# Attention steps of three blocks placed one slot earlier, and the sums of weights cut into four steps instead of three

## The chip, the cores and the metric

The kernel runs on one core of one Trainium2 chip. The metric is the device time of one execution in microseconds (us). The engines are PE (TensorE: matmuls), DVE (VectorE), ACT (ScalarE), POOL (GpSimd) and SP (SyncE, which issues all DMAs here). Each engine works through its own instructions in the order in which they were written down, and waits where an instruction needs something that another engine has not finished.

## The reference

```python
def _attn_ref(q, k, v):                      # B, H, S, D = 8, 8, 576, 64
    ...                                      # cut into chunks of 64 positions
    scores = scale * np.matmul(q_c, k_c.transpose(0, 1, 2, 4, 3))
    scores = scores - np.max(scores, axis=-1, keepdims=True)
    attn = np.exp(scores)
    attn = attn / (np.sum(attn, axis=-1, keepdims=True) + 1e-09)
    out = np.matmul(attn, v_c)
    ...
def _moe_ref(x, w_in, w_out):                # x: 4608 x 512, w_in: 512 x 2048
    h = x @ w_in
    relu6 = np.clip(h + 3.0, 0.0, 6.0)
    g = h * relu6 / 6.0
    return (g @ w_out).astype(np.float32)
```

Chunked attention (64 x 64 blocks) gives the 4608 x 512 matrix x; two large products with a gate between them give the output, all in 32-bit floats.

## The kernel before, in words

The 4608 rows are nine blocks of 512. Every 32-bit product is made of three matmuls: operands are split into a high part and a low part, and `passes` (lines 221 to 223) adds high·high, high·low and low·high.

**Blocks 0 to 2, the standard part.** Here the two products run directly. A `slot` is half a step: an even slot is `mm1`, 12 matmuls of 128x512 into a PSUM tile `h` (two buffers), and an odd slot is `mm2`, 12 matmuls into four `acc` tiles, for the `g` of two steps earlier (`LAG`). There are 96 slots. After `mm1`, ACT makes `r` from `h` (L233), DVE gates it (L234), ACT casts it to `g` (L235) and DVE takes the rest (L236); these four stand in the queues of ACT and DVE in that order.

**Blocks 3 to 8, the Strassen part.** They run in three pairs by one level of a Strassen scheme, which needs sums and differences of quarters of the weights, high and low parts again. These come from `prepare(m, p)`, 16 units (8 values of p, 2 of m) that run during the standard part, in slots 30 to 83. A unit adds high and low part of two weight tiles into the one buffer `a` (two DVE adds, L337), forms four quarters in place (L347, four DVE operations), casts them to the one buffer `hl` (ACT, L350), takes the low part (DVE, L352), and stores four quarters from `hl` to DRAM (L355). It also stores three quarters that need no sum directly from the weight tiles (L333). `hl` and `a` have one buffer each, so the cast of a unit (L350) waits until the four stores of the unit before have landed.

**Attention of blocks 2, 3 and 4** also runs during the standard part, in six pieces (block and half of the heads), put at slots 30, 38, 52, 60, 68 and 76. A piece loads q and k (L142) and v (L147), does 64 small matmuls for the scores (L154), the softmax in four steps (`soft` 0 and 1: row maximum L161 and subtraction L164 on DVE, exponential L165 on ACT; `soft` 2 and 3: sum L168, L169, reciprocal L170, product L172 on DVE), eight transposes on PE (L183) with a copy back by ACT (`e`, L185), and 64 small matmuls for the values (L194), whose result ACT copies out as `x` (L203 or L200). Scores, transposes and values share one PSUM tile, `two`.

**What sets the order.** From slot 30 the order is written out by hand (`manual_schedule`). The table `later` gives each step's distance from the piece's slot. In each slot the matmuls of `mm1` or `mm2` and their ACT and DVE operations come first, then the planned items of that slot, attention ahead of `prepare` (rank 20), then the pending low part L236. A unit of `prepare` starts every third or fourth slot: 30, 33, 36, 40, 43, 46, 50, 53, 57, 60, 63, 67, 70, 73, 77, 80. In slots 43 and 67 `mm2` ends a block, and its four `acc` tiles are emptied by ACT and DVE.

In the text the six pieces are called places 1 to 6, and "mm1(38)", "L185(39)" mean the instruction of that slot.

Of the kernel before, what the change touches and what calls it, by code (L numbers as in the profile page):

```python
# [8 lines left out]
F32 = mybir.dt.float32  # L9
# [21 lines left out]
NFP = NFT // 2  # L31
# [10 lines left out]
def tile_kernel(ctx: ExitStack, tc: tile.TileContext, qk_in, v_in, weights, out):  # L42
    nc = tc.nc
# [45 lines left out]
    words, w, w_h, w_l = {}, {}, {}, {}  # L89
# [28 lines left out]
    def convert_to(ft):  # L118
        nonlocal converted
        load_to(ft + 3)  # L120
        while converted < min(ft, NFT):
            convert(converted)
            converted += 1
# [91 lines left out]
    def finish():  # L215
        while low:
            low.pop(0)()
# [56 lines left out]
    def moe_slots(n, ft, *seg):  # L274

        g = mm1(n, ft)
        yield
        pending.append((n, ft, g, *seg))
        if len(pending) > LAG:
            mm2(*pending.pop(0))  # L280
        yield
# [35 lines left out]
    def kept(m, p, i):  # L317

        if m:
            return stream_b[i, p // 4][:, p % 4]  # L320
        k = ORDER_A.index(i)
        return stream_a[p, k // 4][:, k % 4]

    def quarter(m, row, col):

        return (col, row) if m else (row, col)

    def prepare(m, p):
        cols = lambda k: slice(256 * k, 256 * k + 256)
        for i, row, col in ((1, 0, 0), (2, 0, 1), (4, 1, 1)):  # L330
            f, k = quarter(m, row, col)
            to = kept(m, p, i).rearrange("p (l t) -> p l t", l=2)
            nc.sync.dma_start(out=to, in_=w[p + NFP * f][:, :, m, cols(k)].bitcast(F32))  # L333
        a = sp.tile([P, 2, 512], F32, name="a")
        for f in range(2):
            h, l = [w[p + NFP * f][:, k, m].bitcast(F32) for k in range(2)]
            DVE.tensor_tensor(out=a[:, f], in0=h, in1=l, op=ALU.add)  # L337
        yield

        def q(row, col):  # L340
            f, k = quarter(m, row, col)
            return a[:, f, cols(k)]


        for to, x, y, op in ((q(1, 1), q(1, 0), q(1, 1), ALU.add), (q(1, 0), q(0, 0), q(1, 0), ALU.subtract),
                             (q(0, 0), q(1, 1), q(0, 0), ALU.subtract), (q(0, 1), q(0, 1), q(0, 0), ALU.subtract)):
            DVE.tensor_tensor(out=to, in0=x, in1=y, op=op)  # L347
        hl = sp.tile([P, 2, 2, 2, 256], F32R, name="hl")
        s = a.rearrange("p f (k t) -> p f k t", k=2)
        ACT.copy(out=hl[:, :, :, 0], in_=s)  # L350
        yield
        DVE.tensor_tensor(out=hl[:, :, :, 1], in0=s, in1=hl[:, :, :, 0].bitcast(F32), op=ALU.subtract)  # L352
        for i, row, col in ((5, 1, 1), (7, 1, 0), (6, 0, 0), (3, 0, 1)):
            f, k = quarter(m, row, col)
            nc.sync.dma_start(out=kept(m, p, i), in_=hl[:, f, k].rearrange("p l t -> p (l t)").bitcast(F32))  # L355
        yield


# [4 lines left out]
    def fetch():  # L363
        if stream:
            t, n = stream.pop(0)
            w = wsp.tile([P, 4, 2, 256], F32R, name="ws")
            nc.sync.dma_start(out=w[:, :n].rearrange("p n l t -> p (n l t)").bitcast(F32), in_=t[:, :n].rearrange("p n t -> p (n t)"))
            ahead.append(w)
# [11 lines left out]
    def x_operands(s, eng):  # L380

        n = NSTD + 2 * s
        b = [[xraw[n + j][:, i] for j in range(2)] for i in range(NDP)]
        sub = lambda out, x, y: eng.tensor_tensor(out=out, in0=x, in1=y, op=ALU.subtract)
        ops[s] = {}
        sub(b[0][1], b[0][1], b[0][0])
        for i in ORDER_A:
            ops[s][i] = operand()
            r, c = WHERE[i]
            split(ops[s][i], b[r][c])  # L390

            if i == 5:
                sub(b[0][1], b[1][1], b[0][1])
            elif i == 6:
                sub(b[0][0], b[0][1], b[0][0])
                sub(b[0][1], b[1][0], b[0][1])
            yield
# [3 lines left out]

    plan = {}
    early = [(0, "load_qk"), (1, "load_v"), (2, "scores"), (2, "softmax"), (7, "transpose"), (10, "values")]
    later = [(-2, "load_qk"), (3, "load_v"), (3, "scores"), (4, "soft", 0), (4, "soft", 1), (5, "soft", 2), (5, "soft", 3),
             (8, "transpose"), (9, "values")]

    def put(n, dp, at, steps, stretch=1.0):
        a = Attention(n, dp)
# [7 lines left out]
    SUMS = first[1] + 22  # L416
    FREE = first[3] + 2 * (NFP + LAG + 1)
    for (n, dp), at in zip(((2, 0), (2, 1), (3, 0), (4, 0), (4, 1), (3, 1)), (30, 38, 52, 60, 68, 76)):
        put(n, dp, at, later)
    for u in range(2 * NFP):  # L420
        for k in range(3):
            plan.setdefault(SUMS + u * (FREE - 2 - SUMS) // (2 * NFP) + k, []).append((20, lambda: next(prep)))
    prep = (step for p in range(NFP) for m in range(2) for step in prepare(m, p))
    slot = 0
    sp = made = None
    order = ExitStack()

    for i, (n, lo, hi) in enumerate(SEGMENTS):
        last = all(m != n for m, *_ in SEGMENTS[i + 1:])
        for ft in range(lo, hi):  # L430
            if i == 0:
                convert_to(min(ft + 2, 4))
            elif slot < SUMS:

                with tc.issue_after(second.done.ins):
                    convert_to(5)
                with tc.issue_after(second.last.ins):
                    convert_to(min(6 + 2 * ft, NFT))
            elif slot == SUMS:
                scratch.close()  # L440
                sums = ExitStack()
                sp = sums.enter_context(tc.tile_pool(name="sp", bufs=1, side="right"))
                op = sums.enter_context(tc.tile_pool(name="op", bufs=4, side="right"))
                order.enter_context(tc.manual_schedule())
            for _ in moe_slots(n, ft, ft == lo, ft == hi - 1, not last):
                for _, f in sorted(plan.pop(slot, []), key=lambda s: s[0]):
                    f()
                finish()
                slot += 1
                if slot == FREE:  # L450
                    assert next(prep, None) is None
                    sums.close()
                    op = None
                    start.close()
                    upper.close()
                    xop_pool = pool("xop", 8, side="right")
                    wsp = pool("wsp", 3, side="right")
                    for _ in range(3):
                        fetch()
                    made = x_operands(0, DVE)  # L460
                elif slot > FREE:
                    next(made, None)
# [197 lines left out]
```

## Time and profile before

| what | us |
|---|---|
| median of three runs (lowest, highest) | 855.14 (854.91, 855.72) |
| the profiled execution, whole | 855.06 |
| its span, first to last instruction | 853.1 |
| PE busy in the span | 814.5 |
| DVE busy | 635.8 |
| ACT busy | 369.1 |
| POOL busy | 132.0 |

The span is what the profiler sees between the first and the last instruction; about 2 us of the execution lie outside it. The standard part with the hand-written order begins at 123.9 us (mm1(30)); attention's last values step ends at 322.1 us (slot 85); the Strassen part begins at 354.9 us. In a timeline row stand the start, the duration, the engine, the line, the operation, what is written and read, how many instructions are merged, and in brackets the idle time of that engine just before and what ended it. Matmuls overlap: one of 128x512 has a row of 0.39 us, but the next starts about 0.23 us after it.

### The profile page before, as it was taken

The numbers are of one execution on the slowest core, as the hardware profiler recorded it, in microseconds if no ns is written. First come the engines' busy times: TensorE is split into PE (matmuls) and PEld (weight loads), VectorE is DVE, ScalarE is ACT, GpSimd is POOL, SyncE is SP. The second block draws the span as 40 slices with busy tenths as digits, with TensorE's granted clock in tenths as the row PEclk, the third lists the DMA queues.
The fourth block names the chain that finished last, engine by engine and source line by source line (L and its number), as shares of the span: only waits on it lengthen the run. The fifth ranks groups of instructions, "written<-read, shape, count | busy, mean of one in ns | idle before, by whom it ended". The sixth has DMA issues, their size and how long they took to land.

```text
span 853.1 us, 13690 instructions
## 1 busy us (share of the span) xinstructions
PE 814.5 (95%) x5683; PEld 658.7 (77%) x5683; DVE 635.8 (75%) x768; ACT 369.1 (43%) x455; POOL 132.0 (15%) x77
## 2 busy tenths in 40 slices
PE   7889999789998999999999999999999999999998
PEld 5766878568776777878878888788788887887886
DVE  5978997585866776487699946876899466669951
ACT  4747763243334334334455443344554333336330
POOL 0000000000001000022227002222370022326200
PEclk9898999899999999999999999999999999999999
DMA  9893003856768745166655576666554765555563
GB/s 365 315 360 120 13 0 112 247 184 214 220 187 296 237 160 196 60 232 226 244 189 191 229 254 228 233 214 245 204 192 167 234 226 178 207 186 197 197 212 134
DMA packets 50014, 172.86 MB, mean 203 GB/s; under 512 B 4640, under 2 KB 16928, under 8 KB 39200
## 3 DMA queue, kind: packets, MB, share of 16 engines
q1 hardware_dynamic: 49952, 171.99, 58.0%
q8 instruction: 45, 0.74, 0.3%
q14 instruction: 17, 0.14, 0.1%
HBM read 133.17 MB, written 38.80 MB: 202 GB/s over the span
## 4 chain that ended last, share of the span: by engine, by line
PE 67%; DVE 22%; ACT 5%; issue 3%; DMA 2%; POOL 0%; SPq 0%; ACTq 0%; DVEq 0%
PE acc L221 14%; PE acc L223 14%; PE acc L222 14%; PE h L221 7%; PE h L222 7%; PE h L223 7%; PE two L194 2%; DVE xop L373 2%; DVE m L161 2%; DVE r L234 2%; DVE z L168 1%; DMA w<-w_in_out 1%; DVE a L347 1%; DVE e L164 1%; DVE g L496 1%
## 5 line engine op out<-in xcount | busy, mean ns | idle before, releaser
L221 PE MATMUL acc<-xop,ws 128*128 128x512 f32 x528 | 208.6, 396 | 4.4 <-DVE u L484 4.4
L222 PE MATMUL acc<-xop,ws 128*128 128x512 f32 x528 | 205.8, 390 | 0.0
L223 PE MATMUL acc<-xop,ws 128*128 128x512 f32 x528 | 205.4, 390 | 0.0
L221 PEld LDWEIGHTS acc<-xop,ws 128*128 128x128 f32 x528 | 99.1, 188 | 27.6 <-DVE u L484 6.8
L373 DVE TENSOR_TENSOR xop<-g,xop 128x1024 fp32r<-128x1024 f32 x72 | 103.4, 1468 | 21.5 <-ACT xop L372 21.5
L223 PEld LDWEIGHTS acc<-xop,ws 128*128 128x128 f32 x528 | 99.1, 188 | 20.9
L222 PEld LDWEIGHTS acc<-xop,ws 128*128 128x128 f32 x528 | 99.2, 188 | 19.8
L372 ACT CAST xop<-g 128x1024 fp32r<-128x1024 f32 x72 | 74.4, 1051 | 78.9 <-PE acc L223 51.3
L504 POOL TENSOR_TENSOR g<-g 128x512 f32<-128x512 f32 x24 | 34.8, 1449 | 307.3 <-DVE g L496 307.3
L221 PE MATMUL h<-x,w 128*128 128x512 f32 x192 | 80.0, 419 | 2.1 <-ACT x L203 1.2
L222 PE MATMUL h<-x,w 128*128 128x512 f32 x192 | 78.4, 409 | 0.0
L223 PE MATMUL h<-x,w 128*128 128x512 f32 x192 | 77.8, 405 | 0.0
L222 PE MATMUL acc<-g,w 128*128 128x512 f32 x192 | 75.5, 393 | 0.3 <-DVE g L236 0.3
L221 PE MATMUL acc<-g,w 128*128 128x512 f32 x192 | 75.4, 397 | 0.1
L223 PE MATMUL acc<-g,w 128*128 128x512 f32 x192 | 75.4, 393 | 0.0
L234 DVE SCALAR_TENSOR_TENSOR r<-r,h 128x512 f32<-128x512 f32 x48 | 32.8, 683 | 50.7 <-ACT r L233 50.7
L495 ACT ACTIVATE r<-acc,half 128x512 f32<-128x512 f32 x72 | 48.5, 685 | 26.3 <-DVE acc L484 25.4
L495 ACT ACTIVATE r<-h,half 128x512 f32<-128x512 f32 x24 | 16.5, 687 | 95.0 <-DVE h L484 95.0
L222 PE MATMUL h<-xop,ws 128*128 128x512 f32 x144 | 56.2, 390 | 0.2 <-DVE xop L373 0.2
L221 PE MATMUL h<-xop,ws 128*128 128x512 f32 x144 | 56.3, 391 | 0.0
L223 PE MATMUL h<-xop,ws 128*128 128x512 f32 x144 | 56.1, 389 | 0.0
L496 DVE SCALAR_TENSOR_TENSOR g<-r,acc 128x512 f32<-128x512 f32 x72 | 48.6, 683 | 7.0 <-ACT r L495 6.7
(93 smaller groups left out, 1270.5 us busy)
## 6 DMA issues: line engine op xcount, KB each, us to landing
ws<-b SPq DMA_DIRECT2D x42, 1024.0 KB, 4.8
ws<-a SPq DMA_DIRECT2D x24, 1024.0 KB, 4.9
ws<-a SPq DMA_DIRECT2D x24, 768.0 KB, 4.3
qk<-qk_in SPq DMA_DIRECT2D x17, 1024.0 KB, 6.6
w<-w_in_out SPq DMA_DIRECT2D x16, 1024.0 KB, 13.4
v<-v_in SPq DMA_DIRECT2D x17, 512.0 KB, 5.1
a<-hl SPq DMA_DIRECT2D x32, 256.0 KB, 3.4
b<-hl SPq DMA_DIRECT2D x32, 256.0 KB, 3.4
```

The costliest lines, as they stand in the source:

```text
L161: DVE.tensor_reduce(out=self.m, in_=flat(self.s), axis=AX.X, op=ALU.max)
L164: DVE.tensor_tensor(out=flat(self.e), in0=flat(self.s), in1=wide(self.m), op=ALU.subtract)
L194: PE.matmul(po[o, s, a, i, :], lhsT=self.v[rows, a, i, o], rhs=self.aT[rows, a, i, o], start=True, stop=True)
L221: PE.matmul(ps, lhsT=a_h, rhs=b_h, start=first, stop=False, skip_group_check=more)
L222: PE.matmul(ps, lhsT=a_h, rhs=b_l, start=False, stop=False, skip_group_check=more)
L223: PE.matmul(ps, lhsT=a_l, rhs=b_h, start=False, stop=last, skip_group_check=more)
L234: DVE.scalar_tensor_tensor(out=r, in0=r, scalar=1.0, in1=h, op0=ALU.min, op1=ALU.mult)
L372: ACT.copy(out=t[:, :, 0], in_=src)
L373: DVE.tensor_tensor(out=t[:, :, 1], in0=src, in1=t[:, :, 0].bitcast(F32), op=ALU.subtract)
L495: return (lambda: ACT.activation(out=r, in_=ps, func=AF.Relu, bias=half, scale=1.0 / 6.0), lambda: DVE.scalar_tensor_tensor(out=out, in0=r ...
L496: lambda: DVE.scalar_tensor_tensor(out=out, in0=r, scalar=1.0, in1=ps, op0=ALU.min, op1=ALU.mult))
L504: sub = lambda o, x, y: lambda: POOL.tensor_tensor(out=o, in0=x, in1=y, op=ALU.subtract)
```

## The change

Two things change, both in the standard part.

The table of attention steps: every step comes one slot earlier, so that it falls into a slot of the other kind. The scores come after `mm1` instead of after `mm2`, the transposes at the end of an odd slot (after `mm2`) instead of an even one, and the values at the end of the next even slot. `load_v` keeps its slot and comes behind `soft` 0 and 1.

The units of `prepare`: four steps instead of three. The cast to `hl` (ACT) has a step and a slot of its own, so the cast, the low part and the stores all come one slot later. The three stores of untouched quarters come last in the unit, behind the four stores from `hl`, where they stood first. The starting slots of the units stay.

```diff
     def prepare(m, p):
         cols = lambda k: slice(256 * k, 256 * k + 256)
-        for i, row, col in ((1, 0, 0), (2, 0, 1), (4, 1, 1)):
-            f, k = quarter(m, row, col)
-            to = kept(m, p, i).rearrange("p (l t) -> p l t", l=2)
-            nc.sync.dma_start(out=to, in_=w[p + NFP * f][:, :, m, cols(k)].bitcast(F32))
         a = sp.tile([P, 2, 512], F32, name="a")
...
             DVE.tensor_tensor(out=to, in0=x, in1=y, op=op)
+        yield
         hl = sp.tile([P, 2, 2, 2, 256], F32R, name="hl")
...
             nc.sync.dma_start(out=kept(m, p, i), in_=hl[:, f, k].rearrange("p l t -> p (l t)").bitcast(F32))
+        for i, row, col in ((1, 0, 0), (2, 0, 1), (4, 1, 1)):
+            f, k = quarter(m, row, col)
+            to = kept(m, p, i).rearrange("p (l t) -> p l t", l=2)
+            nc.sync.dma_start(out=to, in_=w[p + NFP * f][:, :, m, cols(k)].bitcast(F32))
         yield
...
-    later = [(-2, "load_qk"), (3, "load_v"), (3, "scores"), (4, "soft", 0), (4, "soft", 1), (5, "soft", 2), (5, "soft", 3),
-             (8, "transpose"), (9, "values")]
+    later = [(-3, "load_qk"), (2, "scores"), (3, "soft", 0), (3, "soft", 1), (3, "load_v"), (4, "soft", 2), (4, "soft", 3),
+             (7, "transpose"), (8, "values")]
...
     for u in range(2 * NFP):
-        for k in range(3):
-            plan.setdefault(SUMS + u * (FREE - 2 - SUMS) // (2 * NFP) + k, []).append((20, lambda: next(prep)))
-    prep = (step for p in range(NFP) for m in range(2) for step in prepare(m, p))
+        unit = prepare(u % 2, u // 2)
+        for k in range(4):
+            plan.setdefault(SUMS + u * (FREE - 2 - SUMS) // (2 * NFP) + k, []).append((20, lambda unit=unit: next(unit)))
```

In the changed file the lines of `prepare` are numbered anew: the adds are L333, the quarters L343, the cast L347, the low part L349, the stores from `hl` L352 and those from the weights L356. All other operations of attention and `mm1`, `mm2` keep their line numbers.

The first place to look at is PE's order around the transposes of place 1, as a piece of the difference. `two` is the PSUM tile of attention, `e` the attention weights, `h` the result of `mm1`, `acc` that of `mm2`.

```order
 L222 MATMUL h<-x,w_1049 128x512
 L223 MATMUL h<-x,w_1049 128x512
-L183 MATMUL two<-ident,e 128x128 x8
+L194 MATMUL two<-e,v 64x64 x32
 L221 MATMUL acc<-g,w_998 128x512
 L222 MATMUL acc<-g,w_998 128x512
```

Behind mm1(38), where the transposes stood, the values now stand; the transposes moved ahead of that mm1. One slot of 12 matmuls lies between transposes and values in both kernels, a `mm2` before and a `mm1` now.

ACT's order at the same place, before, from the exponential of slot 34 to the copy of `x`:

```order
L165 ACTIVATE e_1389<-e_1389 128x1024
L350 CAST hl_1396<-a_1366 128x4x256
L233 ACTIVATE r_1434<-h_1421,half_97 128x512
L235 CAST g_1435<-r_1434 128x512
L350 CAST hl_1464<-a_1444 128x4x256
L233 ACTIVATE r_1479<-h_1466,half_97 128x512
L235 CAST g_1480<-r_1479 128x512
L185 COPY e_1389<-two_1484 128x1024
L203 CAST x_1545<-two_1512 128x2x8x64
```

And in the changed kernel:

```order
L165 ACTIVATE e_1355<-e_1355 128x1024
L233 ACTIVATE r_1384<-h_1371,half_97 128x512
L235 CAST g_1385<-r_1384 128x512
L347 CAST hl_1413<-a_1368 128x4x256
L233 ACTIVATE r_1428<-h_1415,half_97 128x512
L235 CAST g_1429<-r_1428 128x512
L185 COPY e_1355<-two_1457 128x1024
L233 ACTIVATE r_1484<-h_1471,half_97 128x512
L235 CAST g_1485<-r_1484 128x512
L203 CAST x_1522<-two_1489 128x2x8x64
```

Before, the copy L185 stands behind L233 and L235 of the same slot's `mm1` and behind a cast to `hl`; now it stands ahead of the next `mm1`'s L233, and the cast to `hl` ahead of it is that of two slots earlier.

The second place is place 6. ACT before, from the exponential to the copy of `e`:

```order
L165 ACTIVATE e_2829<-e_2829 128x1024
L350 CAST hl_2860<-a_2835 128x4x256
L233 ACTIVATE r_2875<-h_2862,half_97 128x512
L235 CAST g_2876<-r_2875 128x512
L233 ACTIVATE r_2911<-h_2898,half_97 128x512
L235 CAST g_2912<-r_2911 128x512
L185 COPY e_2829<-two_2916 128x1024
```

And in the changed kernel:

```order
L165 ACTIVATE e_2799<-e_2799 128x1024
L347 CAST hl_2804<-a_2726 128x4x256
L233 ACTIVATE r_2819<-h_2806,half_97 128x512
L235 CAST g_2820<-r_2819 128x512
L233 ACTIVATE r_2870<-h_2857,half_97 128x512
L235 CAST g_2871<-r_2870 128x512
L347 CAST hl_2875<-a_2837 128x4x256
L185 COPY e_2799<-two_2890 128x1024
```

Here one more cast to `hl`, that of the last unit, comes to stand directly ahead of the copy L185.

DVE in the changed kernel at place 6, from the row maximum on:

```order
L161 TENSOR_REDUCE m_2797<-two_2747 128x16
L164 TENSOR_TENSOR e_2799<-two_2747,m_2797 128x1024
L234 SCALAR_TENSOR_TENSOR r_2819<-r_2819,h_2806 128x512
L168 TENSOR_REDUCE z_2824<-e_2799 128x16
L169 TENSOR_SCALAR z_2824<-z_2824 128x16
L170 RECIPROCAL z_2824<-z_2824 128x16
L172 TENSOR_TENSOR e_2799<-e_2799,z_2824 128x1024
L349 TENSOR_TENSOR hl_2804<-a_2726,hl_2804 128x4x256
L333 TENSOR_TENSOR a_2837<-w7_823 128x512
L333 TENSOR_TENSOR a_2837<-w15_1049 128x512
L236 TENSOR_TENSOR g_2820<-r_2819,g_2820 128x512
L343 TENSOR_TENSOR a_2837<-a_2837 128x256 x4
```

The low part L349 of the last unit but one stands behind both halves of the softmax's second part, and its stores from `hl` are what the last cast L347 waits for.

More of the change, by code (lines that the diff above doesn't have):

```diff
@@ L450, in tile_kernel @@
                 if slot == FREE:
-                    assert next(prep, None) is None
                     sums.close()
```

## The prediction

> **What bounds the kernel now.** I read the busy times by stretch first, cut where the hand-written order begins, where attention ends and where the Strassen part begins.
>
> ```profile
> core 0: us, PE busy (x) PEld busy (x) DVE busy (x) ACT busy (x) POOL busy (x), PEclk, DMA share, GB/s
> 123.89:322.08 198.19, 180.95 (x1488) 146.09 (x1489) 140.08 (x215) 73.21 (x96) 3.11 (x2) 0.97 0.65 203
> 322.08:354.87 32.79, 32.79 (x151) 27.15 (x145) 20.25 (x22) 15.22 (x20) 0.00 (x0) 1.00 0.29 110
> 354.87:853.00 498.13, 489.83 (x3105) 400.21 (x3103) 370.42 (x411) 200.67 (x249) 127.73 (x68) 1.00 0.60 209
> ```
>
> Only the first stretch is touched. PE is idle there for 198.19 - 180.95 = 17.2 us, and its clock is 0.97. The middle stretch holds ten slots and the two last `mm2`, 12 groups of 12 matmuls without a gap: 32.79 / 12 = 2.73 us for a slot, 0.23 for a matmul. Next PE's row in the waits of the first stretch (us in total, times, longest):
>
> ```profile
> PE two L194 <- ACT e L185: 17.1, 6, 6.4
> ```
>
> All the idle time is one wait: the values' matmuls wait for ACT's copy of the transposed weights, once at each place. PE's timeline shows the six:
>
> ```profile
> 149.82 1.03 PE L183 MATMUL two<-ident,e 128*128 128x128 f32 x8
> 150.62 0.48 PE L221 MATMUL acc<-g,w 128*128 128x512 f32 x1
> ...
> 159.95 1.98 PE L194 MATMUL two<-e,v 64*64 64x64 f32 x64 [6.35 <-ACT e L185]
> ...
> 190.25 1.69 PE L194 MATMUL two<-e,v 64*64 64x64 f32 x64 [2.72 <-ACT e L185]
> ...
> 235.31 1.16 PE L194 MATMUL two<-e,v 64*64 64x64 f32 x64 [1.63 <-ACT e L185]
> ...
> 264.14 1.16 PE L194 MATMUL two<-e,v 64*64 64x64 f32 x64 [2.69 <-ACT e L185]
> ...
> 293.31 1.16 PE L194 MATMUL two<-e,v 64*64 64x64 f32 x64 [1.72 <-ACT e L185]
> ...
> 320.99 1.16 PE L194 MATMUL two<-e,v 64*64 64x64 f32 x64 [2.03 <-ACT e L185]
> 322.08 0.50 PE L221 MATMUL h<-x,w 128*128 128x512 f32 x1
> ```
>
> Transposes occupy PE for 0.80 us (149.82 to 150.62), values for 1.09 (320.99 to 322.08). The clock after such a wait stands in the busy times of the values with the 12 matmuls behind them, at places 1, 2, 4 and 6:
>
> ```profile
> 159.95:165.43 5.48, 5.48 (x76) 4.67 (x77) 1.35 (x2) 1.01 (x1) 0.00 (x0) 0.69 1.01 266
> 190.25:195.76 5.51, 5.50 (x77) 4.64 (x77) 3.03 (x6) 2.06 (x2) 0.00 (x0) 0.69 0.83 242
> 264.14:269.68 5.54, 5.54 (x76) 4.52 (x77) 1.93 (x3) 2.06 (x2) 0.00 (x0) 0.69 1.05 388
> 320.99:324.94 3.95, 3.95 (x77) 3.38 (x77) 0.00 (x0) 1.01 (x1) 0.00 (x0) 1.00 0.48 128
> ```
>
> After waits of 2.69 us and more the granted clock is 0.69 and the same work takes 5.48 to 5.54 instead of 3.95, 1.56 more on average; after 2.03 it is 1.00.
>
> So the six places cost: 17.1 of waiting; 6 x 0.16 = 1.0, since a matmul's row (0.39) counts 0.16 us of drain as busy that the next matmul would have overlapped; 3 x 1.56 = 4.7 of slow clock. Sum **22.8 us**, the most that can be won. Why the copy is late, at place 1 (ACT, with SP's row of the stores from `hl` first):
>
> ```profile
> 149.37 1.79 SPq L355 DMA_DIRECT2D b<-hl  x4
> ...
> 149.97 0.62 ACT L235 CAST g<-r 128x512 fp32r<-128x512 f32 x1 [3.54 <-DVE r L234]
> 155.98 1.04 ACT L350 CAST hl<-a 128x1024 fp32r<-128x1024 f32 x1 [5.39 <-DMA b<-hl]
> 156.93 0.68 ACT L233 ACTIVATE r<-h,half 128x512 f32<-128x512 f32 x1
> 158.37 0.62 ACT L235 CAST g<-r 128x512 fp32r<-128x512 f32 x1 [0.75 <-DVE r L234]
> 158.89 1.01 ACT L185 COPY e<-two 128x1024 f32<-128x1024 f32 x1
> ```
>
> The copy was ready at about 150.8 but stood behind L350, which waited for stores to land, and behind mm1(38)'s L233 and L235, the second of which waits for DVE's L234. Place 6 has no late store, yet waits 2.03: there L233, L234 and L235 of the same slot alone are long.
>
> **The change part by part.** Durations are starts to starts from DVE's and ACT's rows before the last place (the PE row marks the end of an `mm1`):
>
> ```profile
> 304.14 0.39 PE L221 MATMUL acc<-g,w 128*128 128x512 f32 x1
> 305.12 0.69 DVE L234 SCALAR_TENSOR_TENSOR r<-r,h 128x512 f32<-128x512 f32 x1 [2.06 <-ACT r L233]
> 305.73 1.22 DVE L161 TENSOR_REDUCE m<-two 128x16 f32<-128x1024 f32 x1
> 306.98 1.22 DVE L164 TENSOR_TENSOR e<-two,m 128x1024 f32<-128x1024 f32 x1
> 308.12 1.28 DVE L337 TENSOR_TENSOR a<-w 128x512 f32<-128x512 f32 x2
> 308.30 1.06 ACT L165 ACTIVATE e<-e 128x1024 f32<-128x1024 f32 x1 [1.83 <-DVE e L164]
> 309.32 0.68 DVE L236 TENSOR_TENSOR g<-r,g 128x512 fp32r<-128x512 f32 x1
> 309.92 1.21 DVE L168 TENSOR_REDUCE z<-e 128x16 f32<-128x1024 f32 x1
> 311.67 1.22 DVE L172 TENSOR_TENSOR e<-e,z 128x1024 f32<-128x1024 f32 x1
> 312.81 1.80 DVE L347 TENSOR_TENSOR a<-a 128x256 f32<-128x256 f32 x4
> 314.69 1.05 ACT L350 CAST hl<-a 128x1024 fp32r<-128x1024 f32 x1 [5.33 <-DVE a L347]
> 315.64 0.68 ACT L233 ACTIVATE r<-h,half 128x512 f32<-128x512 f32 x1
> 316.35 0.69 DVE L234 SCALAR_TENSOR_TENSOR r<-r,h 128x512 f32<-128x512 f32 x1 [1.74 <-ACT r L233]
> 316.96 1.22 DVE L352 TENSOR_TENSOR hl<-a,hl 128x1024 fp32r<-128x1024 f32 x1
> 318.09 0.69 DVE L236 TENSOR_TENSOR g<-r,g 128x512 fp32r<-128x512 f32 x1
> ```
>
> L234 starts 0.98 after its `mm1` and takes 0.61; L161 1.25; L164 1.14; a pair of adds 1.20; L236 0.60; L168 to L170 1.75; L172 1.14; the four quarters 1.72 (the cast starts 1.88 after them, by the row); the low part 1.13; the cast 0.95 on ACT; L233 to L234 0.71; from place 1 L233 to L235 1.44, L235 to L185 0.52, L185 to values 1.06. Stores from `hl`: four are issued in 1.79 us, the last 1.35 after the first, and
>
> ```profile
> DMA to landing us min/median/max: 2.4/3.4/6.3
> ```
>
> so by the median they land 4.75 us after the first issue; at place 1 it took 6.6 (149.37 to 155.98). I take 5.7, and keep both ends.
>
> *Transposes, place 1.* Zero is the end of mm1(32). PE: scores 1.09, then four slots, mm1(36) done at 12.0, transposes done at 15.5, mm1(38) at 18.3, when the values want `e`. DVE: L234(32) 0.98; L236 waits for L235 and ends at 2.95; L161, L164, low part, adds end at 7.67; L234(34) and second softmax half to 11.17; quarters. ACT: cast of slot 35 at 13.05 (the stores, first issued at 6.6, land at 11.4 to 13.2), L233(36) 14.0, L235(36) 15.45, L185 15.97, values possible at 17.0. That is 1.2 us early: no wait.
>
> *Places 2 to 5*, by the same addition with the pieces of sums that fall in them: place 3, DVE reaches L234(58) at 15.45, L185 at 16.7, values possible 17.75, 0.5 early; places 2 and 5 have 14 us of DVE work in the four slots (place 2 with two copies of `acc`, priced as an add pair), 0.9 early; place 4 is place 1 with two copies of `acc` (ACT, about 1.1 like two L235) ahead of L185, 0.1 early. With errors of about a microsecond on each, some will miss: 0.7 us together, an estimate.
>
> *Place 6.* Zero is the end of mm1(80); mm1(78) ended at -6.55. DVE: L234(78) at -5.57, quarters, L236, L161, L164 done at -0.25. ACT: exponential at -0.07, cast of slot 79 at 0.9, and only then L233(80) at 1.85. DVE: L234(80) 2.56, second softmax half done at 6.06, low part 7.2, first store issued at 7.3, adds, L236, quarters done at 10.7; L234(82) 10.7. ACT: L235(82) 11.4, free at 11.95; the cast of slot 82 needs the stores: landed at 12.05, 13.0 or 13.9 (4.75, 5.7, 6.6). L185 0.95 later, values possible at 14.1, 15.0 or 15.9. PE wants them at 11.7. Wait 2.3, **3.3** or 4.2, where it was 2.03 before. It is past 2.69, so I add the 1.56 of slow clock and 0.16 of drain: 5.0.
>
> The Trainium skill's page "TensorE: Matmul & The Clock Gate" (Part 1: The HAM clock gate) says that the clock drops to half after an idle window of about 3.4 us. By that rule a wait of 3.3 would mostly escape and the sum be 1.6 lower; the rows above, with 0.69 after 2.69 and 2.72, do not agree with it, and I go by them.
>
> *Stores of untouched quarters last.* They stood ahead of a unit's `hl` stores on SP, right behind those of the unit before; now they follow their own. SP's row of stores stays seven in the same cycle, and no engine waits for the three until the weights are fetched back, behind slot 86, a stretch of 32.79 us before the Strassen part. The last three now issue some 10 us later than the last stores before, inside that. Cost zero; lost cover would cost a wait there, at most the few us that one store takes. Moving q, k and v loads by a slot shifts them within the same queue: zero, between a gain and a loss of one store's issue, 0.45 us (1.79 / 4).
>
> *Softmax and cast earlier or later.* DVE has 140.08 us of work in a stretch that would shrink to 175, 80%; no more work is added, and `h` has two buffers, so a late L234 holds PE only when it passes two slots, 5.5 us. Zero.
>
> Sum against the profiled execution: 855.06 - 22.8 + 5.0 + 0.7 = 838.0; the median of the runs is 0.08 above that execution. I predict **838**.
>
> **The rivals.**
> - *Place 6 does not wait either.* Were the stores there early and DVE free 2 us sooner, all 22.8 go: 832.3. Against it: even the early landing leaves 2.3.
> - *DVE's queue still rules.* L235 ahead of the copy waits for L234, which stands behind softmax and sums. If DVE reaches L234 2 us later than my additions at each of places 1 to 5, their waits are 0.8, 1.1, 1.5, 1.9 and 1.1, together 6.4, in place of 0.7: 843.7. For it: place 6 today, without a late store.
> - *The stores take over (slower).* A cast waits for the stores of the unit before, and at places 1, 4 and 6 such a cast, two slots after the low part that it waits for, stands ahead of L185. If the stores land x us after their first issue, values come x - 7.7 us late at place 1 (6.6 + x + 4.0 against 18.3), x - 6.6 at place 4, x - 2.4 at place 6. At x = 14 these are 6.3, 7.4 and 11.6, with 1.72 of clock and drain each 30.5 us, more than the 22.8 won: 862.8. It decides from x = 12. Against it: the longest seen is 6.6.
> - *The change does nothing:* the copy meets another blocker of the same length each time; 855. Nothing in the rows shows one.
>
> **How the numbers follow.** Forecast (835 to 841) 0.58; no wait at all 0.13; DVE's queue 0.21; no effect 0.04; stores, slower 0.04. The range reaches down to 832.3 and up over 843.7 by the end of place 6's landing (0.9): 832 to 845, which leaves the last two cases out and the tails of the others. Two tenths of a per cent, 1.7 us, is about what a measurement can tell from no change: faster 0.92, same 0.04, slower 0.04.
>
> **What would show it.** Right: in the first stretch the wait of L194 for L185 falls from 17.1 to 3 or 4, nearly all at the last place, with the clock at about half behind it and 1.00 elsewhere; the stretch takes 181 us instead of 198, and the Strassen part still 498. Wrong: waits of 1 us or more at places 1 to 5, waits of ACT's casts for stores above 6.6 us, or PE waiting for L234 or for emptied `acc`.

## The result, and the profile after

The changed kernel takes 834.81 us (median of four runs, 834.04 to 836.83), the kernel before 855.38 beside it: a ratio of 0.9764, interval 0.9745 to 0.9782. The forecast was 838 us, between 832 and 845; the measured time lies inside, just below the 835 to 841 that had the largest chance. The profiled execution took 834.43 us, its span is 832.6.

The busy times by the same three stretches (start to end, length, busy time of PE, PEld, DVE, ACT and POOL, granted clock, DMA share, GB/s):

```profile
124.00:301.86 177.86, 175.48 (x1488) 142.62 (x1489) 140.98 (x215) 73.31 (x97) 3.44 (x2) 1.00 0.68 222
301.86:334.51 32.65, 32.65 (x146) 27.03 (x144) 20.25 (x22) 14.21 (x19) 0.00 (x0) 1.00 0.42 143
334.51:832.60 498.09, 489.74 (x3105) 400.13 (x3103) 370.28 (x411) 200.69 (x249) 127.69 (x68) 1.00 0.59 209
```

The first stretch fell from 198.19 to 177.86 us, 20.3 less, at a clock of 1.00 instead of 0.97; the other two kept 32.7 and 498.1. In the waits of that stretch one is left of the six for the copy L185:

```profile
PE two L194 <- ACT e L185: 2.4, 1, 2.4
```

PE's values with ACT's copy ahead of them, at places 1 to 6:

```profile
148.40 1.01 ACT L185 COPY e<-two 128x1024 f32<-128x1024 f32 x1
150.94 1.16 PE L194 MATMUL two<-e,v 64*64 64x64 f32 x64
174.50 1.00 ACT L185 COPY e<-two 128x1024 f32<-128x1024 f32 x1
176.62 1.16 PE L194 MATMUL two<-e,v 64*64 64x64 f32 x64
216.54 1.01 ACT L185 COPY e<-two 128x1024 f32<-128x1024 f32 x1
218.47 1.16 PE L194 MATMUL two<-e,v 64*64 64x64 f32 x64
242.21 1.03 ACT L185 COPY e<-two 128x1024 f32<-128x1024 f32 x1
244.00 1.16 PE L194 MATMUL two<-e,v 64*64 64x64 f32 x64
267.48 1.01 ACT L185 COPY e<-two 128x1024 f32<-128x1024 f32 x1
269.84 1.16 PE L194 MATMUL two<-e,v 64*64 64x64 f32 x64
296.86 1.00 ACT L185 COPY e<-two 128x1024 f32<-128x1024 f32 x1
297.92 1.16 PE L194 MATMUL two<-e,v 64*64 64x64 f32 x64 [2.38 <-ACT e L185]
```

Place 6 shows that values follow 1.06 us after the start of a copy they wait for. At places 1 to 5 they start 2.54, 2.12, 1.93, 1.79 and 2.36 after it: the copy is early by 1.5, 1.1, 0.9, 0.7 and 1.3 us. Place 6 in the queues of DVE, SP and ACT (the PE row marks the end of mm1(80)):

```profile
283.44 0.39 PE L221 MATMUL acc<-g,w 128*128 128x512 f32 x1
...
285.71 0.69 DVE L234 SCALAR_TENSOR_TENSOR r<-r,h 128x512 f32<-128x512 f32 x1 [2.71 <-ACT r L233]
289.21 1.22 DVE L349 TENSOR_TENSOR hl<-a,hl 128x1024 fp32r<-128x1024 f32 x1
290.49 1.80 SPq L352 DMA_DIRECT2D a<-hl  x4
293.99 0.68 DVE L234 SCALAR_TENSOR_TENSOR r<-r,h 128x512 f32<-128x512 f32 x1
294.70 0.62 ACT L235 CAST g<-r 128x512 fp32r<-128x512 f32 x1 [4.79 <-DVE r L234]
295.91 1.04 ACT L347 CAST hl<-a 128x1024 fp32r<-128x1024 f32 x1 [0.58 <-DMA a<-hl]
```

This is the chain that was forecast: L234 of slot 82 behind DVE's backlog, then a cast that waits for stores issued 5.4 us earlier, then the copy.

### The profile page after: what moved, and what is told of

It is laid out like the page before. It is cut to its first block, busy times and chain, and to the rows that moved or that the text cites. A ratio compares the mean times of both kernels' runs of the same rounds, so it can differ in the third digit from the quotient of the medians.

```text
span 832.6 us, 13690 instructions
## 1 busy us (share of the span) xinstructions
PE 808.9 (97%) x5683; PEld 655.1 (79%) x5683; DVE 636.6 (76%) x768; ACT 368.2 (44%) x455; POOL 132.3 (16%) x77
## 4 chain that ended last, share of the span: by engine, by line
PE 77%; DVE 14%; ACT 3%; issue 3%; DMA 2%; POOL 0%; SPq 0%; ACTq 0%; DVEq 0%
PE acc L221 17%; PE acc L223 16%; PE acc L222 16%; PE h L221 8%; PE h L222 8%; PE h L223 8%; DVE xop L374 2%; PE two L194 2%; DMA w<-w_in_out 1%; DVE g L496 1%; PE two L154 1%; DVE u L108 1%; PE two L183 1%; DVE u L484 1%; ACT r L495 1%
## 5 line engine op out<-in xcount | busy, mean ns | idle before, releaser
L221 PE MATMUL h<-x,w 128*128 128x512 f32 x192 | 77.8, 407 | 2.1 <-ACT x L203 1.1
L222 PE MATMUL h<-x,w 128*128 128x512 f32 x192 | 77.1, 402 | 0.0
L223 PE MATMUL h<-x,w 128*128 128x512 f32 x192 | 76.6, 399 | 0.0
L495 ACT ACTIVATE r<-h,half 128x512 f32<-128x512 f32 x24 | 16.5, 687 | 94.1 <-DVE h L484 94.1
L234 DVE SCALAR_TENSOR_TENSOR r<-r,h 128x512 f32<-128x512 f32 x48 | 32.8, 682 | 32.3 <-ACT r L233 32.2
L233 ACT ACTIVATE r<-h,half 128x512 f32<-128x512 f32 x48 | 32.9, 686 | 47.8 <-PE h L223 47.3
```

What stands on the lines that cost most here:

```text
L221: PE.matmul(ps, lhsT=a_h, rhs=b_h, start=first, stop=False, skip_group_check=more)
L222: PE.matmul(ps, lhsT=a_h, rhs=b_l, start=False, stop=False, skip_group_check=more)
L223: PE.matmul(ps, lhsT=a_l, rhs=b_h, start=False, stop=last, skip_group_check=more)
L233: ACT.activation(out=r, in_=h, func=AF.Relu, bias=half, scale=1.0 / 6.0)
L234: DVE.scalar_tensor_tensor(out=r, in0=r, scalar=1.0, in1=h, op0=ALU.min, op1=ALU.mult)
L495: return (lambda: ACT.activation(out=r, in_=ps, func=AF.Relu, bias=half, scale=1.0 / 6.0), lambda: DVE.scalar_tensor_tensor(out=out, in0=r ...
```

## The experiments

The theory: what cost time was what stands ahead of the copy L185 in ACT's queue, and what is left at place 6 is the same. The first rival: the new cutting of the sums brings the gain by itself.

**The attention table alone**, the sums as before (in the kernel before, only the lines of `later` are replaced):

```diff
-    later = [(-2, "load_qk"), (3, "load_v"), (3, "scores"), (4, "soft", 0), (4, "soft", 1), (5, "soft", 2), (5, "soft", 3),
-             (8, "transpose"), (9, "values")]
+    later = [(-3, "load_qk"), (2, "scores"), (3, "soft", 0), (3, "soft", 1), (3, "load_v"), (4, "soft", 2), (4, "soft", 3),
+             (7, "transpose"), (8, "values")]
```

> The new table of attention steps with the sums of weights as before (three steps, stores of untouched quarters first). Theory (the gain is the place of ACT's copy L185 in its queue): most of the gain stays, but the casts to hl now stand in other slots, directly ahead of the copy at places 2 and 5, two slots behind the stores they wait for; by the prediction's addition waits of about 3.3 us at place 2, 2.2 at place 5, 1.0 at place 6, none at the others: 6.5 us in all instead of 2.4, so 839 us (837 to 842). Rival (the four steps of the sums bring the gain): 853 to 855.

Measured: 841.39 us, ratio 0.9833 (0.9816 to 0.9849); inside the expected time, but the waits are spread otherwise. The rival falls. PE's remaining waits for the copy at places 2, 5 and 6:

```profile
179.15 1.16 PE L194 MATMUL two<-e,v 64*64 64x64 f32 x64 [0.81 <-ACT e L185]
275.86 1.71 PE L194 MATMUL two<-e,v 64*64 64x64 f32 x64 [3.44 <-ACT e L185]
303.46 1.16 PE L194 MATMUL two<-e,v 64*64 64x64 f32 x64 [0.35 <-ACT e L185]
```

Place 5 waits because a cast to `hl` stands directly ahead of the copy and its stores, issued at 267.41 with a load of q and k right behind them, let it start only 6.4 us later:

```profile
267.41 1.80 SPq L355 DMA_DIRECT2D a<-hl  x4
269.31 0.50 SPq L142 DMA_DIRECT2D qk<-qk_in  x1
...
273.85 1.04 ACT L350 CAST hl<-a 128x1024 fp32r<-128x1024 f32 x1 [3.45 <-DMA a<-hl]
274.80 1.01 ACT L185 COPY e<-two 128x1024 f32<-128x1024 f32 x1
```

PE has two more waits here that the expectation did not name, for DVE's low part of `x` (L206) and for DVE's emptying of `acc` (L264); the changed kernel has neither:

```profile
158.52 1.16 PE L154 MATMUL two<-qk 64*64 64x64 f32 x64 [0.64 <-DVE x L206]
173.00 0.50 PE L221 MATMUL acc<-g,w 128*128 128x512 f32 x1 [0.65 <-DVE o L264]
```

So the table alone brings 14.0 of the 20.6 us.

**The sums alone**, attention as before (in the changed kernel, only the lines of `later` are put back):

```diff
-    later = [(-3, "load_qk"), (2, "scores"), (3, "soft", 0), (3, "soft", 1), (3, "load_v"), (4, "soft", 2), (4, "soft", 3),
-             (7, "transpose"), (8, "values")]
+    later = [(-2, "load_qk"), (3, "load_v"), (3, "scores"), (4, "soft", 0), (4, "soft", 1), (5, "soft", 2), (5, "soft", 3),
+             (8, "transpose"), (9, "values")]
```

> The sums in four steps with their untouched stores last, attention's steps as before. Theory: the copy still stands behind L233 and L235 of its own slot; only the cast to hl that waited for stores directly ahead of it at place 1 is gone, so place 1 waits about 3 us instead of 6.35 and the others about 2 each as before: about 851 us (848 to 854). Rival (the sums bring the gain): 835 to 838.

Measured: 857.8 us, ratio 1.0021 (1.0010 to 1.0033): the rival falls, and the theory's number was also too low. The six waits for the copy remain, 16.3 us in all against 17.1 before. Place 1 fell to 2.19, but place 5 rose from 1.72 to 4.18, since the cast of the slot before the transposes now waits there for stores, as ACT's rows at place 5 show:

```profile
285.59 0.62 ACT L235 CAST g<-r 128x512 fp32r<-128x512 f32 x1 [4.58 <-DVE r L234]
289.50 1.04 ACT L347 CAST hl<-a 128x1024 fp32r<-128x1024 f32 x1 [3.29 <-DMA a<-hl]
290.45 0.68 ACT L233 ACTIVATE r<-h,half 128x512 f32<-128x512 f32 x1
```

Added up, the waits for the copy are shorter than before, so they are not what makes this kernel slower. Its profiled execution took 858.75 us, 3.7 more than that of the kernel before, and the first stretch shows where (PE's row in its waits, its busy times, and one row of PE):

```profile
PE two L194 <- ACT e L185: 16.3, 6, 4.2
123.83:325.53 201.70, 184.47 (x1488) 149.46 (x1488) 141.35 (x215) 72.71 (x96) 3.46 (x2) 0.95 0.61 196
...
174.73 0.50 PE L221 MATMUL acc<-g,w 128*128 128x512 f32 x1 [0.98 <-ACT o L266]
```

PE's busy time for the same matmuls is 184.47 us instead of 180.95, at a clock of 0.95 instead of 0.97: the clock dropped behind four of the six waits (2.19, 3.37, 2.40 and 4.18 us), before behind three. PE also waited once, 0.98 us, for ACT's emptying of `acc`.

The two halves do not add: the sums alone lose about 2 us, and on top of the new table they win 841.39 - 834.81 = 6.6. The profiles show most of it at place 5: the cast that stands directly ahead of the copy with the table alone, and makes PE wait 3.44 us with a slow clock behind (5.51 us for the values and 12 matmuls), comes a slot later in the changed kernel, where place 5 has no wait and takes 3.99.

**The stores of untouched quarters first again**, all else as changed:

```diff
+        for i, row, col in ((1, 0, 0), (2, 0, 1), (4, 1, 1)):
...
         a = sp.tile([P, 2, 512], F32, name="a")
...
-        for i, row, col in ((1, 0, 0), (2, 0, 1), (4, 1, 1)):
...
         yield
```

> The changed kernel with the stores of untouched quarters first in a unit again. Theory: SP's queue is the same cycle of seven stores, the cast of place 6 waits as long as now: 834.8 us, within 1 us, and a wait of about 2.4 us at place 6. Rival (their place matters, since they can delay the stores from hl): the landing of those stores grows by up to the 1.8 us that three stores take to issue, place 6 waits 4 us, 836.5 us or more.

Measured: 834.65 us, ratio 0.9751 (0.9737 to 0.9766), a wait of 1.83 us at place 6 and 0.20 at place 4. The place of these stores makes no difference to the time that can be measured, and the wait at place 6 is shorter, not longer; the rival falls.

**Only ACT's order, in the kernel before**: in the six slots with transposes the gate of that slot's `mm1` is written behind the copy.

```diff
+        def gate():
+            ACT.activation(out=r, in_=h, func=AF.Relu, bias=half, scale=1.0 / 6.0)
...
+        if slot in TRANSPOSES:
+            plan[slot].append((7.5, gate))
+        else:
+            gate()
...
+    TRANSPOSES = (38, 46, 60, 68, 76, 84)
```

> The kernel before with one edit: in the six slots that hold the transposes, L233, L234 and L235 of that slot's mm1 are written behind the copy L185 instead of ahead of it. PE's order, the attention table and the sums stay as before. Theory (the copy's place in ACT's queue is what costs): waits vanish at places 3 to 6, place 2 keeps about 0.4 us, place 1 keeps about 4.4 us since a cast that waits for stores still stands ahead of the copy: 839 us (837 to 842). Rival (the slot's kind, or DVE's lag, decides): at least 850.

Measured: 842.59 us, ratio 0.9845 (0.9830 to 0.9859), just above the expected range; the rival falls. With PE's order, the table and the sums untouched, 12.8 us are won by what stands ahead of one instruction, six times. What stays are 4.09 us at place 1 (expected 4.4), 0.27 at place 2 (0.4) and 1.59 at place 5 (none expected): there the cast ahead of the copy waits 1.14 us for DVE's quarters, which I had not counted (with the added lines the cast is L357 and the quarters are L354 in this kernel):

```profile
PE two L194 <- ACT e L185: 6.0, 3, 4.1
281.67 1.04 ACT L357 CAST hl<-a 128x1024 fp32r<-128x1024 f32 x1 [1.14 <-DVE a L354]
```

**The last unit's cast behind the copy**, in the changed kernel:

```diff
-            plan.setdefault(SUMS + u * (FREE - 2 - SUMS) // (2 * NFP) + k, []).append((20, lambda unit=unit: next(unit)))
+            plan.setdefault(SUMS + u * (FREE - 2 - SUMS) // (2 * NFP) + k + (u == 15 and k > 1), []).append((20, lambda unit=unit: next(unit)))
```

> The changed kernel with one edit: the cast to hl, the low part and the stores of the last unit come one slot later, so that the cast of slot 82 stands behind the copy L185 of place 6 instead of ahead of it. Theory (at place 6 the copy waits for L235, late by DVE's queue, and then for that cast and its stores): the copy starts 0.5 us after L235 of slot 82, 1.6 us earlier than now, and place 6 waits 0.7 us instead of 2.4: 833.2 us, 1.6 less than the changed kernel. Rival (DVE's queue alone makes the copy late): no gain, 834.8 us and a wait of 2.4 us.

Measured: 832.95 us, ratio 0.9732 (0.9716 to 0.9748), and at place 6

```profile
295.91 0.62 ACT L235 CAST g<-r 128x512 fp32r<-128x512 f32 x1 [4.79 <-DVE r L234]
296.44 1.01 ACT L185 COPY e<-two 128x1024 f32<-128x1024 f32 x1
297.50 1.16 PE L194 MATMUL two<-e,v 64*64 64x64 f32 x64 [0.75 <-ACT e L185]
```

The wait is as expected to 0.05 us; the rival falls. So 1.6 us of the 2.4 were the cast with its stores, 0.75 is DVE's lag: the copy now follows L235 directly, and L235 waits for DVE's L234.

**The last two units one slot earlier**, in the changed kernel:

```diff
-            plan.setdefault(SUMS + u * (FREE - 2 - SUMS) // (2 * NFP) + k, []).append((20, lambda unit=unit: next(unit)))
+            plan.setdefault(SUMS + u * (FREE - 2 - SUMS) // (2 * NFP) + k - (u > 13), []).append((20, lambda unit=unit: next(unit)))
```

> The changed kernel with one edit: the last two units of sums start one slot earlier (76 and 79 instead of 77 and 80), so that place 6 gets the pattern of place 1: cast of the last unit in slot 81, an odd slot, and DVE's quarters done before L234 of slot 82. Theory: no wait at place 6, 2.4 us less and 0.16 of drain: 832.3 us, 2.5 less than the changed kernel on the same chip. Rival (any order leaves one such place, since a unit pressed into earlier slots makes place 5 late): the wait moves to place 5, 834 us or more.

**The changed kernel again**, on the same chip:

> The changed kernel itself once more, to be set beside the two kernels above on the same chip: 834.8 us (834 to 836), a wait of about 2.4 us (1.8 to 2.6) at place 6 and below 0.3 us elsewhere.

Measured: 832.97 us for the earlier units, ratio 0.9731 (0.9716 to 0.9745), and 835.86 for the changed kernel, ratio 0.9767 (0.9752 to 0.9781). The intervals do not meet: with two units started a slot earlier the kernel is 2.9 us faster than the change, as fast as the one with the last cast behind the copy (832.95). The rival falls: PE waits for no copy in it, and place 6's values start without a wait:

```profile
294.23 1.01 ACT L185 COPY e<-two 128x1024 f32<-128x1024 f32 x1
...
296.42 1.16 PE L194 MATMUL two<-e,v 64*64 64x64 f32 x64
```

From mm1(30) to the values of place 6 the profiles of the three kernels took 173.89 us (changed), 172.27 (last cast behind the copy) and 171.45 (earlier units): 1.6 and 2.4 less, as the two theories expected. The medians differ by more, 2.9 both times. A slow clock of about 1.6 us behind place 6, which of these three profiles only that of the changed kernel has, can account for the rest; one execution of each kernel was profiled, so this is not shown for the others.

The changed kernel's second profile also answers the question of the clock. Its wait at place 6 is as long as in the first profile (2.35 against 2.38), but the values with the 12 matmuls behind them took 3.94 us at a clock of 1.00 in the first (first row) and 5.54 at 0.69 in the second:

```profile
297.92:301.86 3.94, 3.94 (x76) 3.38 (x77) 1.67 (x3) 2.07 (x3) 0.00 (x0) 1.00 0.55 194
```

```profile
297.79:303.33 5.54, 5.54 (x76) 4.53 (x77) 1.68 (x3) 2.08 (x3) 0.00 (x0) 0.69 0.77 265
```

**More ACT work ahead of the copy**, in the changed kernel; seven copies, later five and six:

```diff
+    pad = const.tile([P, NB, CH], BF16, name="pad")
...
+            if self.n in (2, 3, 4):
+                for _ in range(7):
+                    ACT.copy(out=pad, in_=self.e[:, 0])
             ACT.copy(out=self.aT, in_=tp)
```

> The changed kernel with seven more ACT copies of 128x512 (one half of e, to a tile that nobody reads) directly ahead of the copy L185 at each of the six places, 0.53 us each, 3.7 us in all. It measures how early the copy now is. Theory, with the 1.5, 1.1, 0.9, 0.7 and 1.3 us by which the copy ended before the values' start at places 1 to 5 in the trace: waits of 2.2, 2.6, 2.8, 3.0, 2.4 and, at place 6, 6.1 us; the clock at about half behind some of the waits over 2.2 us and behind all over 2.7; with drain and 1.6 us for each of four to six drops, 858 us (855 to 862), above the kernel before. Rival (the copy has more room than the trace shows, or the values wait for something else as well): less than half of it, below 846 us.

Measured (one run): 864.8 us, where the kernel before took 855.89; above the expected range, on the theory's side. The seven copies take 4.55 us, not 3.7; less the room of places 1 to 5, and added to the 2.38 of place 6, that gives 3.1, 3.5, 3.7, 3.8, 3.3 and 6.9. PE's rows (with the added lines the copy is L189 and the values are L198 in this kernel):

```profile
154.61 1.16 PE L198 MATMUL two<-e,v 64*64 64x64 f32 x64 [3.00 <-ACT e L189]
183.79 1.99 PE L198 MATMUL two<-e,v 64*64 64x64 f32 x64 [3.43 <-ACT e L189]
230.78 1.46 PE L198 MATMUL two<-e,v 64*64 64x64 f32 x64 [3.61 <-ACT e L189]
261.69 1.61 PE L198 MATMUL two<-e,v 64*64 64x64 f32 x64 [3.75 <-ACT e L189]
292.23 1.46 PE L198 MATMUL two<-e,v 64*64 64x64 f32 x64 [3.13 <-ACT e L189]
326.22 1.98 PE L198 MATMUL two<-e,v 64*64 64x64 f32 x64 [6.75 <-ACT e L189]
```

Each is within 0.2 us of that: at all six places the values wait for the copy alone, and putting work ahead of it takes the whole gain away and more. Behind the 3.00 us at place 1 the clock stayed at 1.00 (3.96 us for the values and 12 matmuls), against the theory's drop behind every wait over 2.7.

The same with five copies, twice, and with six:

> As the kernel with seven copies, with five: 0.65 us each by the row of that one, 3.25 us in all. Waits by the room read from the trace: 1.8, 2.2, 2.4, 2.5 and 2.0 us at places 1 to 5, 5.6 at place 6. If the length of the wait decides over the clock (a limit near 2.6 us), it drops at place 6 alone: 848 us. If where the wait falls decides between about 2.1 and 2.6 us, some of places 2 to 4 drop and some do not, 1.5 us each: 849 to 853 us.

> The kernel with five copies once more. If the length of the wait decides, the same places drop as in the run before it; if where it falls decides, other places drop at the same length of wait.

> With six copies, 3.9 us in all: waits of 2.4, 2.8, 3.0, 3.2, 2.6 and 6.3 us. Places 2, 3, 4 and 6 drop by either reading (all waits seen at 2.69 us and more did); places 1 and 5 tell the readings apart: both or neither by length, either by where it falls. 855 to 859 us.

Measured (one run each, the kernel before at 856.88 beside them): 856.99, 855.5 and 860.59 us; above the expected 853 and 859. The 848 of the first expectation did not follow from its own waits: they are 14.1 us longer than the 2.4 of the changed kernel, which with one drop of 1.6 makes 834.8 + 14.1 + 1.6 = 850.5. And the slow clock at place 6 cost more than 1.6: the values with the 12 matmuls took 6.43 and 6.80 us there with five copies, 2.5 and 2.9 more than at full clock. The third expectation's remark that all waits of 2.69 us and more had dropped was wrong, by the 3.00 above.

The waits with five copies were the same in both executions, 1.71, 2.13, 2.31, 2.46 or 2.47, 1.83, and 5.42 or 5.48. The clock was not. Values and 12 matmuls at places 3 and 5, of the first execution and then of the second:

```profile
227.73:233.21 5.48, 5.48 (x76) 4.68 (x77) 3.94 (x6) 2.10 (x3) 0.00 (x0) 0.69 0.60 229
286.62:290.62 4.00, 4.00 (x77) 3.39 (x77) 2.48 (x4) 3.02 (x4) 0.00 (x0) 1.00 0.01 4
```

```profile
227.50:231.45 3.95, 3.95 (x77) 3.39 (x78) 2.40 (x3) 2.10 (x3) 0.00 (x0) 1.00 0.50 201
283.29:288.83 5.54, 5.54 (x77) 4.52 (x77) 3.63 (x5) 3.02 (x4) 0.00 (x0) 0.69 0.25 91
```

After 2.31 us at place 3 the first dropped and the second did not; after 1.83 at place 5 the second dropped and the first did not. With six copies the clock dropped behind waits of 2.36, 2.49 and 2.96 us, and not behind 2.78 and 3.12. Length alone does not decide.

## Why the prediction was right, and where a term was off

- **The bound of 22.8 us** (17.1 of waiting, 1.0 of drain, 4.7 of clock) held: the first stretch lost 20.3, and that is 17.1 - 2.4 of waiting, 5 x 0.16 of drain and the 4.7 of clock, together 20.2.
- **Places 1 to 5 free of waits**: right. The room forecast for the copy was 1.2, 0.9, 0.5, 0.1 and 0.9 us, measured 1.5, 1.1, 0.9, 0.7 and 1.3: the chains were 0.2 to 0.6 too long each. The 0.7 us set aside for misses there was not needed.
- **Place 6 waits**: right in kind and mechanism, 3.3 us forecast, 2.38 measured in this profile, within its two ends of 2.3 and 4.2. Counted from the end of mm1(80) at 283.44, the first store was issued at 7.05, not 7.3, and the cast started 5.4 after it, not 5.7, so values were possible at 14.5, not 15.0; and PE's last matmul ahead of them ended at 12.1, not 11.7 (0.16 of that is the drain, which the prediction counted apart). The kernel with the last cast behind the copy split it into 1.6 for cast and stores and 0.75 for DVE's lag.
- **The clock behind place 6** is the term that was mis-sized. The prediction put 1.56 us there with certainty, since waits of 2.69 and more had dropped and 2.03 had not. The profiled execution had none, the second profile of the same kernel had 1.6 after the same wait; that the first had none is chance. The forecast was 3.2 too high: 1.6 by this term, 0.9 by the wait at place 6 and 0.7 by the misses set aside. Without that term, with 2.5 for place 6's wait and drain, and nothing for misses, the sum is 855.06 - 22.8 + 2.5 = 834.8.
- On the Trainium skill's page "TensorE: Matmul & The Clock Gate" (Part 1): it states that the window in which activity is judged is free-running, and the two executions with five copies agree, 2.31 us with and without a drop. Its figure of an idle window of about 3.4 us before a drop does not fit: a wait of 1.83 us was followed by one.
- **Stores last cost nothing**: right, 834.65 with the stores first again. That the loads of q, k and v, moved by a slot, cost nothing either was not tested by itself. What the prediction did not see is that the sums in four steps gain only with the new table; it summed the two halves together only, and the kernel with the sums alone is 0.2% slower than before, while the table alone gains 14.0 us.
- The rivals: that no wait at all would be left did not come here, though a shift of two units brings it; DVE's queue left 0.75 us at one place; the stores were only part of place 6; that the change does nothing is ruled out by the 20.6 us.

## What to carry to other kernels

When a matmul waits for a small copy, read the queue of the engine that makes the copy: what stands ahead of it, and what that waits for, is the price, and the copy's place can be changed without touching a matmul. Instructions with a late input from DMA (here the cast into a single buffer) belong behind such a copy, and moving only the cast, with the copy left where it was, gained nothing here (857.8 against 855.43). Write the room of each place down as a chain of start times; here that gave the room to within 0.6 us and pointed to the place that was left.

## What the runs showed of the hardware

TensorE's clock after a wait is partly chance: the same wait in the same kernel was followed by a drop in one execution and not in the other. Over all profiles here, none of the 11 waits for the copy up to 1.72 us was followed by a lower clock, 14 of the 24 between 1.83 and 3.13 us were, and all 12 from 3.37 us on. A drop cost 1.5 to 1.6 us in the values and 12 matmuls behind a wait of 1.8 to 3.1 us, and 1.5 to 2.9 behind longer ones. So one execution's profile cannot price it: the same kernel shows it in one profile and not in the next.
